# One load queue, moved warm-up matmuls and fewer weight-rest transfers in the head of a fused attention and MLP kernel

## The chip, the cores and the metric

One core of a Trainium2 chip runs one launch of the kernel. The metric is device time in microseconds (us) of that launch; lower is better. A profiled execution also has a span, from the first to the last instruction of the program; the device time of the same execution is somewhat longer than its span.

## The reference

The input x has 2048 tokens of width 448. It is layer-normalised, and the normalised xn goes two ways: through a linear attention of 16 heads (head width 28) and through a squared-ReLU MLP of width 1792. The result is x + s * silu(mlp).

```python
xn = _layernorm(x, axis=-1)
# attention
qkv = (xn @ wqkv)                      # 448 -> 3 * 448, 16 heads of 28
phi = lambda t: jnp.where(t > 0, t + 1, jnp.exp(t)) + 1e-6
pq, pk = phi(q), phi(k)
kv = jnp.einsum("bhsd,bhse->bhde", pk, v)
num = jnp.einsum("bhqd,bhde->bhqe", pq, kv)
den = jnp.einsum("bhqd,bhd->bhq", pq, z)[..., None] + 1e-6     # z: sum of pk over tokens
s = (num / den).reshape(B, S, D) @ wo
# MLP
h = xn @ w1 + b1
g = silu((relu(h) ** 2) @ w2 + b2)
return x + s * g
```

All tensors are bfloat16 in memory.

## The kernel before

The 2048 tokens are 16 tiles of 128 (names end in the tile number `si`), in four groups of four tiles (`g` = 0 to 3). The width 448 is cut into three chunks of 128 and a rest of 64; the rest chunk of a weight is kept in both partition halves (`HALF[0]`, `HALF[1]`), so that two matmuls of 64 rows can run side by side in the two halves of the array.

The code is a recorder with a planner. `add` records an operation with its reads, its writes and an estimated duration; `place` (the planner) puts the operations of ScalarE, VectorE and GpSimd in an order by its own estimate of time and picks one of eight PSUM banks for each buffer; `emit` writes the instructions with semaphore waits. TensorE (PE) and SyncE (SP) are FIXED: they run in the order of the program text. So the text order of loads is the order on SP's queue, and the order on VectorE (DVE) and ScalarE (ACT) follows from the planner's estimates, in which `prio`, `lead`, `after` and the `rate` of a load are inputs. Once emitted, every engine's order is fixed: an instruction that waits holds everything behind it on its engine.

The stage that the change touches is the first 23 us:

- **Loads.** `load_x(lo, hi)` loads token tiles into `x_tok`; `load_rows` loads 128 rows of the first 768 columns of w1 (part "w1a", chunk c); `load_rest` loads the 64 rest rows of some columns into one half; `load_main` loads the three full chunks of a column range. Parts "w1b" and "w1c" are columns 768 to 1280 and 1280 to 1792 of w1; "wk" and "wq" are the key and query columns of wqkv. The ACT queue carries b1 and the w1a rows of chunk 0, SP all the rest.
- **Norms.** For each of tiles 0 to 3: `ln_stats` (bn_stats L420 and bn_aggr L423 on DVE), `ln_rstd` (two activations on ACT, L428 and L432), `ln_norm` (DVE L438). The planner puts statistics of tile 1 ahead of the norm of tile 0 on DVE.
- **Head of the MLP.** `warm(8)` and two more `warm` calls (L990) are matmuls of ones whose result nobody reads. `tile_transpose(si)` transposes xn by PE (L482), with copies to `xT` on DVE or ACT (L490). `h_part(si, c)` (L1008) adds chunk c of tile si to six PSUM buffers, `heads[0..5]`, which hold the first six blocks of h for 512 tokens. `h_rests` (L1023) adds the rest rows, and `h_out` evacuates each head by a ReLU (ACT L606 or DVE L603).
- **Bursts.** `fours("H6 H7|H8 H9", 0)` and the like (L624 for H units, L564 for K, L588 for Q) run four units in two pairs, each pair in two PSUM banks: first four steps of the first pair, then four of the second, then three of each. H8 is block 8 of h, K0 the keys of tile 0, Q0 block 0 of the queries; a stroke, as in H3', means the next group of tokens. So H7 and H9 begin 8 matmuls after H6 and H8, and need two banks that earlier units have left.
- **Group 1.** `ln_group(1)` norms tiles 4 to 7 in two pairs, each pair followed by one DMA transpose (SP, L467) to `xT`. Its first reader on PE is H3' in `fours("Q0 Q1|Q2 H3'", 0)`, which needs all four tiles. `hold` makes statistics wait: tiles 4 and 5 for the last PE copy of tile 3, tiles 6 and 7 for the ReLU of head 2 (`relus[0, 2]`).

Of the kernel before, what the change touches and what calls it, by code (L numbers as in the profile page):

```python
# [9 lines left out]
P = 128  # L10
S, D, F = 2048, 448, 1792
# [231 lines left out]
def bass_recurrent_scan__linear_attn_block__dense_activation_squared_relu__prompt_kernel(  # L243
    nc, A_x, A_wqkv, A_wo, B_x, B_w1, B_b1, B_w2, B_b2, out
):
    with ExitStack() as es:
        sb = lambda name, shape, dtype: es.enter_context(nc.sbuf_tensor(name, shape, dtype))
        bf, f32 = dt.bfloat16, dt.float32
        pr = Program()
# [10 lines left out]
        xT = sb("xT", [P, NT, 4, P], bf)  # L260
        w_qkv = sb("w_qkv", [P, 4, 3 * D + 16], bf)
        w_1 = sb("w_1", [P, 4, F], bf)
# [6 lines left out]
        mv = sb("mv", [P, NT, 2], f32)  # L269
        rstd = sb("rstd", [P, NT], f32)  # L270
# [19 lines left out]
        FULL, HALF = slice(0, 128), (slice(0, 64), slice(64, 128))  # L290
# [51 lines left out]
        def dma(eng, dst, src, writes, nbytes, reads=(), after=(), prio=None, rate=None):  # L342
            return add(
                eng, lambda e, _: e.dma_start(dst, src), reads, writes, 0.45 if eng == "sp" else 0.5, nbytes=nbytes,
                after=after, prio=prio, mode=rate or 270e3,
            )

        def load_x(lo, hi, rate=None):
            dma(
                "sp", x_tok[:, lo:hi, :], x_r[:, lo:hi, :], [("x", i) for i in range(lo, hi)], (hi - lo) * P * D * 2,  # L350
                rate=rate,
            )

        def load_main(w, src, name, lo, hi):
            dma(
                "sp", w[:, 0:3, lo:hi], src[0:384, lo:hi].rearrange("(c p) j -> p c j", p=P), [(name, "m")],
                768 * (hi - lo),
            )

        def load_rest(eng, w, src, name, half, lo, hi, prio=None):  # L360
            dma(eng, w[HALF[half], 3, lo:hi], src[384:448, lo:hi], [(name, half)], 128 * (hi - lo), prio=prio)

        add("act", lambda e, _: e.preload_act_table_set("natural_log_exp_and_others"), [], ["actw"], 0.05, prio=-9)
        def load_rows(eng, c, prio=None, rate=None):
            dma(
                eng, w_1[:, c, 0:768], B_w1[c * P : (c + 1) * P, 0:768], [("w1a", "m", c)], 768 * 256, prio=prio,
                rate=rate,
            )

        dma("act", b1r[:, :], B_b1.rearrange("(f p) -> f p", p=P), ["b1r"], F * 2, prio=-8.5)  # L370
        load_x(0, 1)
        load_rows("act", 0, -8, rate=170e3)
        load_x(1, 2, rate=160e3)
        load_rows("sp", 1, rate=560e3)
        load_x(2, 3, rate=280e3)
        load_x(3, 4, rate=280e3)
        load_rows("sp", 2)
        load_rest("sp", w_1, B_w1, "w1a", 0, 0, 384)
        load_rest("sp", w_1, B_w1, "w1a", 1, 384, 768)
        for name, lo in (("w1b", 768), ("w1c", 1280)):  # L380
            load_main(w_1, B_w1, name, lo, lo + 512)
            load_rest("sp", w_1, B_w1, name, 0, lo, lo + 256)
            load_rest("sp", w_1, B_w1, name, 1, lo + 256, lo + 512)
            if name == "w1b":
                load_x(4, 8)
        load_main(w_qkv, A_wqkv, "wk", D, 2 * D)
        load_rest("sp", w_qkv, A_wqkv, "wk", 0, D, 2 * D)
        load_rest("sp", w_qkv, A_wqkv, "wk", 1, D, 2 * D)
        load_main(w_qkv, A_wqkv, "wq", 0, D)
        load_rest("sp", w_qkv, A_wqkv, "wq", 0, 0, D)  # L390
        load_rest("sp", w_qkv, A_wqkv, "wq", 1, 0, D)

        def load_b2():
            src = bass.AP(tensor=B_b2.tensor, offset=B_b2.offset, ap=[[0, P], [1, D]])
# [17 lines left out]
            load_rest("sp", w_qkv, A_wqkv, "wv", 1, 2 * D, 3 * D)  # L412

        masks()
        W = lambda name: [(name, k) for k in ("m", 0, 1)]


        def ln_stats(si, prio=None, after=()):
            add(
                "dve", lambda e, _: e.bn_stats(st6[:, si, :], x_tok[:, si, :]), [("x", si)], [("st", si)], 0.53 if prio is None else 0.63,  # L420
                prio=prio, after=after,
            )
            add("dve", lambda e, _: e.bn_aggr(mv[:, si, :], st6[:, si, :]), [("st", si)], [("mv", si)], 0.07, prio=prio and (0.0, 0.3, 0.3, -0.5, 2.7)[prio])  # L423
# [30 lines left out]
        def ln_group(g, lead=(1.8, 0.0), between=None):  # L454
            for a in (4 * g, 4 * g + 2):
                if a % 4 and between:
                    between()
                hold = [relus[0, 2] if a == 6 else pr.writer[("xT", 3, 1)]]
                ln_stats(a, after=hold)
                ln_stats(a + 1, after=hold)  # L460
                ln_rstd(a, a + 2)
                ln_norm(a)
                ln_norm(a + 1)
                ln_twin(a, a + 2)
                add(
                    "sp",
                    lambda e, _, a=a: e.dma_start_transpose(  # L467
                        xT[:, a : a + 2, :, :].rearrange("p s c t -> p (s c) t"),
                        xn[:, a : a + 2, :].rearrange("p s d -> p (s d)"),
                    ),  # L470
                    [(n, i) for n in ("xn", "xd") for i in (a, a + 1)], [("xT", a), ("xT", a + 1)], 1.25,
                    nbytes=2 * P * 1024, mode=180e3, lead=lead[a % 4 // 2],
                )
# [21 lines left out]
        def tile_transpose(si):  # L495
            pe_transpose([(si, 0)], [("xn", si)], xT[:, si, 0:1, :], ("xT", si, 0), ("dve", "act"), 0)
            pe_transpose([(si, 1), (si, 2)], [("xn", si)], xT[:, si, 1:3, :], ("xT", si, 1), ("act", "dve"), 0.2)
# [36 lines left out]
        def xt_names(lo, n):  # L534
            out = []
            for i in range(lo, lo + n):
                out += [("xT", i, 0), ("xT", i, 1), "xT3"] if i < 4 else [("xT", i)]
            return out
# [21 lines left out]
        def kk(si):  # L560
# [20 lines left out]

            return Unit(b, xt_names(si, 1) + W("wk"), mm, done)

        def qq(g, m):
# [8 lines left out]
            done = lambda: phi(b, pqT[:, m, g * 512 : (g + 1) * 512], ("pq", g, m), 512)  # L593
            return Unit(b, xt_names(4 * g, 4) + W("wq"), mm, done)

        relus = {}
# [20 lines left out]
        HLO, HHI = (0, 1, 2, 6, 7, 10, 11), (3, 4, 5, 8, 9, 12, 13)  # L617

        def hh(g, fi):
            b = Buf("H")  # L620
            ts = slice(4 * g, 4 * g + 4)

            def mm(e, rows, c, start, stop):
                return e.matmul(  # L624
                    ps(b)[:, 0:512].rearrange("p (s t) -> p s t", t=P), w_1[rows, c, fi * P : (fi + 1) * P],
                    xT[rows, ts, c, :], start=start, stop=stop,
                )

            part = "w1a" if fi < 6 else "w1b" if fi < 10 else "w1c"
            reads = xt_names(ts.start, ts.stop - ts.start) + [(part, 0 if fi in HLO else 1)]  # L630
            reads += [("w1a", "m", c) for c in range(3)] if fi < 6 else [(part, "m")]
            return Unit(b, reads, mm, lambda: h_out(b, g, fi))

# [351 lines left out]
        def warm(n, after=(), cols=512):  # L985
            b = Buf("W")

            def f(e, _):
                for _i in range(n):
                    last = e.matmul(ps(b)[:, 0:cols], one[:, 0:P], one[:, 0:cols], start=True, stop=True)  # L990
                return last

            add("pe", f, list(after), [b], n * cols / 1280, mode="128")
# [9 lines left out]
        def h_part(si, *chunks):  # L1003
            for c in chunks:

                def f(e, _, c=c):
                    for fi, b in enumerate(heads):
                        last = e.matmul(  # L1008
                            ps(b)[:, si * P : (si + 1) * P], w_1[:, c, fi * P : (fi + 1) * P], xT[:, si, c, :],
                            start=(si == 0 and c == 0), stop=False, skip_group_check=True,  # L1010
                        )
                    return last

                reads = [("xT", si, min(c, 1)), ("w1a", "m", c)] + (heads if si or c else [])
                add("pe", f, reads, heads, 6 * 0.056, mode="128")
# [19 lines left out]
        def b1_rows():  # L1035
            b = Buf("B1")
            add(
                "pe",
                lambda e, _: e.transpose(ps(b)[:, 0 : NF // 2].bitcast(bf), b1r[:, :], ident[0:NF, 0:NF]),
                ["b1r", "ident"], [b], 0.06, mode="128",  # L1040
            )
            add(
                "act",
                lambda e, _: e.activation(out=b1f[:, :], in_=ps(b)[:, 0 : NF // 2].bitcast(bf), func=AF.Copy), [b],
                ["b1f"], 0.15, prio=0.1,
            )

        warm(8)
        b1_rows()
        warm(4, [("mv", 0)], P)  # L1050
        warm(3, [("rstd", 0)], P)
        tile_transpose(0)
        h_part(0, 0)
        tile_transpose(1)
        h_part(0, 1)
# [8 lines left out]
        h_part(3, 0, 1, 2)  # L1064
        h_rests()
        load_w2(0, 5, [pr.writer["xT3"]])
        ln_group(1, (4.0, 4.0))
        load_w2(5, 14)
        load_b2()
        load_x(8, 12)  # L1070
# [79 lines left out]
```

## Time and profile before

| | us |
|---|---|
| median of three runs | 145.04 |
| the three runs | 144.49, 145.04, 145.11 |
| the profiled execution, device time | 144.88 |
| its span | 143.2 |
| PE busy in the span | 139.3 |
| DVE busy | 91.8 |
| ACT busy | 77.4 |
| GpSimd (POOL) busy | 27.0 |

The profile has a page and several views of one trace. In the chain of waits each line has a start, a duration, and what the end of the kernel depended on in that stretch. In the timeline each line is a run of instructions: start, duration, engine, line of the code, what is written and read, a count, and in brackets how long the engine was idle before it and what ended that. SPq and ACTq rows are issues of DMAs; PEld is the load of a matmul's stationary operand, which runs beside PE. The list of DMA issues gives size and time from issue to landing. The table by windows gives busy time and instruction count of an engine in a stretch, then the granted clock of TensorE, the busy share of the DMA engines and GB/s.

### The profile page before, as it was taken

How to read it: one execution, taken by the hardware profiler on the slowest of the kernel's cores; microseconds unless marked ns; L12 is line 12 of the kernel's file. 1: busy time of each engine (PE TensorE's matmuls, PEld its weight loads, DVE VectorE, ACT ScalarE, POOL GpSimd, SP SyncE). 2: the span in 40 equal slices, each digit the busy share in tenths (PEclk: the TensorE clock that was granted, in tenths of full speed). 3: DMA queues.
4: the chain of work that ended last, by engine and by line, in shares of the span. 5: the costliest groups of instructions: out<-in, count | busy, mean ns of one | idle time of the engine just before them, and what ended most of it. 6: DMA issues, size and time to landing. Idle time of an engine off the chain costs nothing.

```text
span 143.2 us, 3283 instructions
## 1 busy us (share of the span) xinstructions
PE 139.3 (97%) x1343; PEld 71.8 (50%) x1343; DVE 91.8 (64%) x224; ACT 77.4 (54%) x151; POOL 27.0 (19%) x46
## 2 busy tenths in 40 slices
PE   7999999999999999999999999999999999999992
PEld 2597444444554445445446444445544555554561
DVE  1757999989994655365264779700248929367963
ACT  3244999997715286527417999475179430303020
POOL 7200003514000504103200651000000005041520
PEclk9999999999999999999999999999999999999999
DMA  3889799990436000000000000013992001203242
GB/s 100 252 259 299 205 166 281 287 342 19 78 73 146 0 5 0 0 5 0 0 0 5 0 2 5 0 36 96 190 187 46 7 0 32 96 5 128 64 135 58
DMA packets 18322, 12.90 MB, mean 90 GB/s; under 512 B 7572, under 2 KB 17924, under 8 KB 18308
## 3 DMA queue, kind: packets, MB, share of 16 engines
q1 hardware_dynamic: 17060, 11.56, 29.9%
q10 hardware_dynamic: 1248, 1.15, 4.0%
q8 instruction: 10, 0.16, 0.5%
q14 instruction: 4, 0.03, 0.1%
HBM read 9.16 MB, written 1.97 MB: 78 GB/s over the span
## 4 chain that ended last, share of the span: by engine, by line
PE 94%; DMA 2%; DVE 1%; SPq 0%; issue 0%; ACT 0%
PE pb L624 27%; PE pb L877 26%; PE pb L564 7%; PE pb L686 6%; PE pb L588 6%; PE pb L947 6%; PE pb L1008 4%; PE pb L900 4%; DMA x_tok<-in_A_x_dram 2%; PE pb L974 1%; PE pb L660 1%; PE pb L691 1%; PE pb L482 1%; PE pb L817 1%; PE pb L737 1%; PE pb L842 1%
## 5 line engine op out<-in xcount | busy, mean ns | idle before, releaser
L606 ACT ACTIVATE r<-pb,b1f 128x512 bf16<-128x512 f32 x54 | 35.2, 691 | 21.0 <-PE pb L624 19.9
L624 PE MATMUL pb<-xT,w 64*128 64x512 bf16 x350 | 46.2, 376 | 0.0
L877 PE MATMUL pb<-w,r 64*128 64x448 bf16 x392 | 38.9, 349 | 0.0
L612 DVE TENSOR_TENSOR r<-r 128x512 bf16<-128x512 bf16 x40 | 17.9, 471 | 19.0 <-ACT r L606 19.0
L624 PEld LDWEIGHTS pb<-xT,w 64*128 64x128 bf16 x350 | 18.7, 94 | 19.5 <-DVE pqT L552 0.3
L877 PEld LDWEIGHTS pb<-w,r 64*128 64x128 bf16 x392 | 19.0, 94 | 18.4 <-PE pb L842 0.4
L576 POOL TENSOR_TENSOR zacc<-zacc,pk 128x448 f32<-128x448 f32 x13 | 13.7, 1050 | 47.5 <-DVE pk L552 47.0
L864 ACT ACTIVATE gbuf<-gbuf 128x448 bf16<-128x448 bf16 x15 | 8.1, 579 | 22.0 <-DVE gbuf L858 20.2
L936 POOL TENSOR_TENSOR gbuf<-gbuf,x_tok 128x448 bf16<-128x448 bf16 x7 | 7.2, 1032 | 44.1 <-DVE gbuf L932 44.0
L932 DVE TENSOR_TENSOR gbuf<-pb,gbuf 128x448 bf16<-128x448 f32 (+2 forms) x17 | 9.2, 591 | 9.0 <-PE pb L947 7.5
L564 PE MATMUL pb<-w_qkv,xT 64*128 64x448 bf16 x112 | 14.5, 349 | 0.0
L588 PE MATMUL pb<-xT,w_qkv 64*128 64x512 bf16 x84 | 14.2, 376 | 0.0
L420 DVE BATCH_NORM_STATS2 st<-x_tok 128x6 f32<-128x448 bf16 x16 | 9.5, 613 | 4.9 <-DMA x_tok<-in_A_x_dram 4.9
L613 ACT ACTIVATE r<-r 128x512 bf16<-128x512 bf16 x16 | 9.8, 633 | 0.3
L552 DVE SCALAR_TENSOR_TENSOR pk<-pb,pk 128x448 bf16<-128x448 f32 x16 | 9.4, 616 | 0.1
L686 PE MATMUL pb<-pk,xn 128*128 128x448 bf16 x48 | 9.4, 353 | 0.0
L858 DVE TENSOR_TENSOR gbuf<-pb,b2b 128x448 bf16<-128x448 f32 x15 | 8.7, 614 | 1.0 <-PE pb L877 0.6
L564 PEld LDWEIGHTS pb<-w_qkv,xT 64*128 64x128 bf16 x112 | 6.1, 94 | 5.6
L552 DVE SCALAR_TENSOR_TENSOR pqT<-pb,pqT 128x512 bf16<-128x512 f32 x12 | 8.2, 689 | 0.3
L947 PE MATMUL pb<-msb,pqT 64*128 64x448 bf16 x72 | 8.3, 349 | 0.0
L542 ACT ACTIVATE pk<-pb 128x448 bf16<-128x448 f32 x16 | 7.9, 546 | 0.5 <-PE pb L624 0.5
L588 PEld LDWEIGHTS pb<-xT,w_qkv 64*128 64x128 bf16 x84 | 5.3, 94 | 5.0 <-DVE pqT L552 0.4
(81 smaller groups left out, 123.8 us busy)
## 6 DMA issues: line engine op xcount, KB each, us to landing
out_dram<-gbuf SPq DMA_DIRECT2D x15, 112.0 KB, 1.8
x_tok<-in_A_x_dram SPq DMA_DIRECT2D x3, 448.0 KB, 8.1
w_qkv<-in_A_wqkv_dram SPq DMA_DIRECT2D x3, 336.0 KB, 7.6
w<-in_B_w_dram SPq DMA_DIRECT2D x1, 1008.0 KB, 6.1
w<-in_B_w_dram SPq DMA_DIRECT2D x2, 384.0 KB, 5.4
w_o<-in_A_wo_dram SPq DMA_DIRECT2D x1, 672.0 KB, 10.2
r<-rden_scratch SPq DMA_DIRECT2D x6, 112.0 KB
w<-in_B_w_dram SPq DMA_DIRECT2D x1, 560.0 KB, 7.5
```

The lines of the kernel that those rows point to most:

```text
L420: "dve", lambda e, _: e.bn_stats(st6[:, si, :], x_tok[:, si, :]), [("x", si)], [("st", si)], 0.53 if prio is None else 0.63,
L552: lambda e, _: e.scalar_tensor_tensor(out=slot, in0=ps(buf)[:, 0:n], scalar=1.0 + 1e-6, in1=slot, op0=ALU.add, op1=ALU.max),
L564: return e.matmul(ps(b)[:, 0:D], xT[rows, si, c, :], w_qkv[rows, c, D : 2 * D], start=start, stop=stop)
L576: return e.tensor_tensor(out=o[:, dst : dst + n], in0=first[:, src : src + n], in1=pk[:, si, src : src + n], op=ALU.add)
L588: return e.matmul(ps(b)[:, 0:512].rearrange("p (s t) -> p s t", s=4), w_qkv[rows, c, m * P : (m + 1) * P], xT[rows, 4 * g : 4 * g + 4, c, ...
L606: return e.activation(out=slot, in_=ps(b)[:, 0:512], func=AF.Relu, bias=b1f[:, fi : fi + 1])
L612: return e.tensor_tensor(out=slot, in0=slot, in1=slot, op=ALU.mult)
L613: return e.activation(out=slot, in_=slot, func=AF.Square)
L624: return e.matmul(ps(b)[:, 0:512].rearrange("p (s t) -> p s t", t=P), w_1[rows, c, fi * P : (fi + 1) * P], xT[rows, ts, c, :], start=start ...
L686: last = e.matmul(ps(b)[:, 0:D], xn[:, si, c * P : (c + 1) * P], pk[:, si, :], start=(si == 0), stop=(si == NT - 1),)
L877: last = e.matmul(ps(b)[:, 0:D], r2[si // 4][HALF[h], fi, t], w_2[HALF[h], fi, :], start=(part == 0 and fi == 0), stop=(part == 1 and fi = ...
L947: return e.matmul(ps(b)[:, 0:D], ap[c][rows, :], msb[rows, c, :], start=start, stop=stop)
```

## The change

```diff
         load_x(0, 1)
-        load_rows("act", 0, -8, rate=170e3)
-        load_x(1, 2, rate=160e3)
-        load_rows("sp", 1, rate=560e3)
+        load_x(1, 2, rate=250e3)
+        load_rows("sp", 0, rate=250e3)
+        load_rows("sp", 1, rate=330e3)
         load_x(2, 3, rate=280e3)
         load_x(3, 4, rate=280e3)
         load_rows("sp", 2)
         load_rest("sp", w_1, B_w1, "w1a", 0, 0, 384)
         load_rest("sp", w_1, B_w1, "w1a", 1, 384, 768)
-        for name, lo in (("w1b", 768), ("w1c", 1280)):
-            load_main(w_1, B_w1, name, lo, lo + 512)
-            load_rest("sp", w_1, B_w1, name, 0, lo, lo + 256)
-            load_rest("sp", w_1, B_w1, name, 1, lo + 256, lo + 512)
-            if name == "w1b":
-                load_x(4, 8)
+        load_main(w_1, B_w1, "w1b", 768, 1280)
+        for h in (0, 1):
+            src = B_w1[384:448, 768:1792].rearrange("p (b j) -> p b j", j=256)[:, h::2, :]
+            dst = w_1[HALF[h], 3, 768:1792].rearrange("p (b j) -> p b j", j=256)[:, h::2, :]
+            dma("sp", dst, src, [("w1r", h)], 128 * 512)
+        load_x(4, 8)
+        load_main(w_1, B_w1, "w1c", 1280, 1792)
         load_main(w_qkv, A_wqkv, "wk", D, 2 * D)
-        load_rest("sp", w_qkv, A_wqkv, "wk", 0, D, 2 * D)
-        load_rest("sp", w_qkv, A_wqkv, "wk", 1, D, 2 * D)
+        load_rest("sp", w_qkv, A_wqkv, "wqk", 0, 0, 2 * D)
+        load_rest("sp", w_qkv, A_wqkv, "wqk", 1, 0, 2 * D)
         load_main(w_qkv, A_wqkv, "wq", 0, D)
-        load_rest("sp", w_qkv, A_wqkv, "wq", 0, 0, D)
-        load_rest("sp", w_qkv, A_wqkv, "wq", 1, 0, D)
...
-                hold = [relus[0, 2] if a == 6 else pr.writer[("xT", 3, 1)]]
-                ln_stats(a, after=hold)
-                ln_stats(a + 1, after=hold)
+                ln_stats(a, after=[relus[0, 2] if a == 6 else pr.writer[("xT", 3, 1)]])
+                ln_stats(a + 1, after=[relus[0, 2]])
...
         warm(8)
+        warm(3, [("mv", 0)], P)
         b1_rows()
-        warm(4, [("mv", 0)], P)
-        warm(3, [("rstd", 0)], P)
+        warm(2, [("rstd", 0)], P)
         tile_transpose(0)
+        warm(3, cols=P)
         h_part(0, 0)
...
-        ln_group(1, (4.0, 4.0))
+        ln_group(1, (7.0, 5.0))
```

The names that the readers wait for follow: an H unit of w1b or w1c now waits for ("w1r", half), K and Q units wait for ("wqk", half). The w1a rows of chunk 0 move from ACT's queue to SP's, third in line. SP issues 17 loads up to and with wq instead of 19, ahead of the first part of w2. The w1 rests of both parts stand ahead of tiles 4 to 7 in the queue, and the query rests ahead of the query main part.

In the emitted order of the changed kernel, DVE runs for group 1: statistics and aggregate of tile 4, the ReLUs of heads 3 and 1, statistics and aggregate of tile 5, statistics of tiles 6 and 7, norms of tiles 4 and 5 and their copy, aggregates of 6 and 7, three squares, norms of 6 and 7 and their copy. Before, it was: statistics of 4 and 5, a ReLU, two aggregates, a ReLU, statistics of 6 and 7, two aggregates, norms of 4 and 5 and their copy, one square, norms of 6 and 7 and their copy. On ACT the second activation of tile 0's rstd now stands ahead of the copy of b1, and ACT runs four ReLUs ahead of the rstd of tiles 4 and 5 and three more ahead of that of tiles 6 and 7 (before, three, with one between the two activations, and one). The PE order differs in the warm-up matmuls alone: 3, 2 and 3 of 128 columns in place of 4 and 3. H6 and H8 now take banks 5 and 6, H7 and H9 banks 2 and 7; bank 2 held head 3, whose ReLU is the first of the two on DVE. From the first gates on, the order of all engines is nearly that of before.

More of the change, by code (lines that the diff above doesn't have):

```diff
@@ L414, in bass_recurrent_scan__linear_attn_block__dense_activation_squared_relu__prompt_kernel @@
         masks()
-        W = lambda name: [(name, k) for k in ("m", 0, 1)]
+        W = lambda name: [(name, "m")] + [("wv" if name == "wv" else "wqk", h) for h in (0, 1)]
         def ln_stats(si, prio=None, after=()):
@@ L629, in hh @@
             part = "w1a" if fi < 6 else "w1b" if fi < 10 else "w1c"
-            reads = xt_names(ts.start, ts.stop - ts.start) + [(part, 0 if fi in HLO else 1)]
+            reads = xt_names(ts.start, ts.stop - ts.start) + [(part if fi < 6 else "w1r", 0 if fi in HLO else 1)]
             reads += [("w1a", "m", c) for c in range(3)] if fi < 6 else [(part, "m")]
```

## The prediction

> **What bounds the kernel now.** The page gives the bound of the whole:
>
> ```profile
> span 143.2 us, 3283 instructions
> ...
> PE 94%; DMA 2%; DVE 1%; SPq 0%; issue 0%; ACT 0%
> ```
>
> PE carries 94% of the chain of waits, and no PE instruction behind the head goes away. So the change can only move the point from which PE runs without a break, and any later wait of PE caps that. The chain in order of time shows its start:
>
> ```profile
> 1.26 3.12 DMA x_tok<-in_A_x_dram
> ...
> 4.41 0.64 DVE st L420
> ...
> 6.20 0.82 PE pb L1008 x6
> ```
>
> Tile 1 lands at 4.38, 3.12 us after its issue; its statistics stand ahead of tile 0's norm on DVE, and from them norm, transpose and copy lead to the first h matmul at 6.20. The windows then show the clock:
>
> ```profile
> 6.20:10.03 3.83, 3.83 (x37) 1.00 0.78 223
> 10.03:12.90 2.87, 2.87 (x51) 1.00 0.90 293
> ```
>
> 37 matmuls of 128 columns take 3.83 us (104 ns each), the next 51 take 2.87 (56 ns). The granted clock says 1.00 in both, but PE runs at half rate until 10.03. The timeline shows the next place where PE could stop:
>
> ```profile
> 12.54 1.15 DVE L420 BATCH_NORM_STATS2 st<-x_tok 128x6 f32<-128x448 bf16 x2 [0.83 <-DMA x_tok<-in_A_x_dram]
> ...
> 13.61 0.73 DVE L603 TENSOR_SCALAR r<-pb,b1f 128x512 bf16<-128x512 f32 x1
> 14.26 0.24 DVE L423 BATCH_NORM_AGGREGATE mv<-st 128x2 f32<-128x6 f32 x2
> 14.40 2.72 PEld L624 LDWEIGHTS pb<-xT,w 64*128 64x128 bf16 x28 [0.30 <-DVE r L603]
> ```
>
> DVE idles until tiles 4 to 7 land (12.52), runs two statistics, then the ReLU that frees a bank for H7; that weight load goes at 14.40 and PE's 14.43 matmul follows its predecessor without a gap. **The bank arrives at the moment PE wants it.** So PE may come earlier as it likes: without an earlier landing of tiles 4 to 7, or less DVE work ahead of the ReLU, H7 stays where it is. The DMA issues have the last place, one line per transfer:
>
> ```profile
> x_tok<-in_A_x_dram SPq DMA_DIRECT2D x1, 448.0 KB, 5.9
> ...
> xT<-xn SPq DMA_TRANSPOSE x1, 3.8
> ...
> xT<-xn SPq DMA_TRANSPOSE x1, 3.3
> ```
>
> The transposes of tiles 4 to 7 are issued at 17.25 and 18.65 and land at 21.04 and 21.93; their reader H3' starts at 23.12, so 1.2 us are spare.
>
> **The change, part by part.** All against the profiled execution: 144.88 us device time, 143.2 span, so 1.7 lie outside; it stands 0.16 below the median of 145.04.
>
> *Chunk 0 of w1a behind tile 1 on SP.* Today ACT issues it at 1.51 beside tile 1 (1.26). In the landing counts of the trace, 15 of tile 1's 16 shares are in by 3.49 and one at 4.38: that one shared its DMA engine with packets of the ACT queue that took 0.63 to 0.75 us. On one queue these packets come behind it. Bounds for tile 1: 3.4 (SP's issue step of 0.46 behind tile 0's landing at 2.98) to 4.38; I take 3.5, by the 15 shares. DVE is busy with tile 0 until 3.84, so statistics of tile 1 start at 3.86 in place of 4.41: 0.55 earlier, and by the same steps (1.79 us from there) the first h matmul is ready at 5.65. Chunk 0 itself, issued at 1.73 for 1.51, lands after 3.4 us as now, 5.1 at the latest: 0.5 spare. Tiles 2 and 3, chunks 1 and 2 and the w1a rests are each issued 0.46 later; the tightest, chunk 2 (6.60, read at 8.5 now), keeps over 0.9 us.
>
> The Trainium skill, page "DMA: Bandwidth & Descriptors", section "Issuing engines are not separate DMA queues", speaks against this part: transfers from different issuers run on the same DMA engines, so that choosing the issuer saves only issue time. By it tile 1 would stay at 4.38 and the 0.55 would be 0; by the row above the late share is the shared engine's, and I keep 0.55. The sum by it is 144.9.
>
> *Warm-up matmuls.* Eight of 128 columns for seven: one more of 107 ns (the half-rate spacing, 0.93 us for 7 with starts 107 apart). The three behind tile 0's transposes run while PE would wait for the copy (0.29 us, 5.91 to 6.20 now): at half rate 3 x 0.107 = 0.32, so 0.03 longer than the cover, at full rate hidden. The one wait that moves is b1's transpose, 0.32 us later behind the three: b1 is first read at 13.34. In return ACT runs tile 0's second rstd step at 4.19 for 4.65; it is hidden, as tile 0's norm waits for tile 1's statistics.
>
> What they do to the clock this trace can't show; it shows full rate 3.83 us after the last PE gap. With gaps filled, bounds: full rate from 0.84 + 3.83 = 4.7 (gaps no longer count) to 10.03 (no effect). I take 3.83 after the last gap of the new order (at 5.04, before tile 0's transposes): 8.9. The work from 6.20 to 14.42 is 3.83 at half rate, 2.0 at full, and 4.39 at full: 6.4 us. From 5.68, with 3.2 at half rate (worth 1.67) and 4.7 left, PE would reach H7 at 13.6; bounds 12.1 (all at full rate) and 14.15 (10.03 again), against 14.42.
>
> The skill, "TensorE: Matmul & The Clock Gate", section "The HAM clock gate", has a free-running activity window of 3.4 us and warns against fitting to a cold count, since the switch moves from run to run; the 10.03 agrees with such a window. By that page my estimate is a switch anywhere from about 4.3 to 7.7 with PE full from 0.84, and PE at H7 still earlier; the bank decides all the same.
>
> *Rests in fewer transfers.* SP saves two issues (w1 rests, 0.5 to 0.6 each) behind tiles 4 to 7 and two (wqkv rests) behind "wk". But tiles 4 to 7 themselves are issued one step later (0.46, chunk 0's), behind 64 KB more of rests. Price of those 64 KB: the same amount took 0.38 today (w1b landed at 9.05, its two rests by 9.43). Most shares of tiles 4 to 7 land by 11.2, the last two at 12.48 and 12.52, one behind a single packet of 1.14 us. Landing of tiles 4 to 7: at worst 12.52 + 0.46 + 0.38 = 13.4, at best without that late packet 11.5. **I take 12.77**: the two delays overlap on the late DMA engines, which are not waiting for issues there, and part of the bad luck will not recur. Key rests: wqkv rests bring 112 KB more ahead of K0, w1 rests 64 less, so 48 KB net (0.16 at some 300 GB/s) on 16.0 plus 0.25: 16.4, needed at 17.45. Query columns land at 18.3 now, needed 22.25: hidden. The first part of w2 (20.1, read at 31.3) as well.
>
> *Statistics of one tile ahead of the ReLUs.* From the landing L: 0.02 to start, 0.66 to the aggregate, 0.10 to the ReLU's start, 0.73 for it, 0.06 to the weight load: **L + 1.57**, now L + 1.88. With 12.77 that is 14.34 against 14.40: 0.06 to 0.08 gained. This ReLU now also waits for an aggregate that waits for its statistics; behind it stand the second ReLU (its bank is read 2.2 us later) and the rest of the group's norms.
>
> *Norms of tiles 4 to 7.* By the same spacings (statistics 0.53, ReLU 0.65, aggregate 0.10, norm 0.28 and 0.39, copy 0.2, square 0.335): first transpose issued at L + 4.83 (now L + 4.74), second at L + 6.84 (now 6.13), as three squares and, on ACT, three ReLUs stand ahead. It lands 3.3 later at L + 10.1; H3' wants it at L + 1.57 + 8.70 = L + 10.3. The 1.2 us spare shrink to 0.1 or 0.2: hidden, barely. SP is held by that transpose up to about 20.9 in place of 19.95, and with it w2's second part (landed 26.1, read near 34), b2, tiles 8 to 15 (29.4 and 30.6, read at 51 and later): all spare.
>
> **Sum.** PE is at H7 by 13.6, the bank comes at 14.34 to 14.40, later waits add nothing: 0.08 gained of 144.88, so **144.8 us**, no change beyond 0.5% (0.72 us), which is about what a measurement of this kernel can tell, as its three runs lie 0.62 apart.
>
> **Rivals.**
>
> 1. *Tiles 4 to 7 land early and the clock is early.* For: only a few of 16 shares were late, one by one packet. Against: the late ones stayed late in all following loads. Landing at 11.7 puts the bank at 13.3; PE must be there by then, so full rate before about 8.3. The cap is K0 at 16.4: 1.05 of 17.45. Time 144.88 - 1.05 = 143.8. Chance 0.24.
> 2. *H3' takes the wait over, slower.* Place: the second transpose of group 1, PE at Q0. For: its slack falls from 1.2 to under 0.2, and it stands behind a ReLU on ACT that needs H7's end. Against: each step was hidden so far. It decides from an issue later than L + 7.0. If it is issued 0.5 later, lands after 3.8 as the first does now, and tiles 4 to 7 come at 13.1: 13.1 + 7.34 + 3.8 = 24.24 against 23.12, so 1.1 slower: 146.0. Chance 0.21.
> 3. *Tile 1 does not land earlier and the warm-up does nothing.* For: no row shows the late share gone, nor a switch at another time. Against: the late share waited behind packets that now come after it. PE then reaches H7 at 14.45 and the result is 144.9, inside the forecast's class. Chance 0.07; the forecast itself has 0.48.
>
> **How the numbers follow.** Within 0.5% are forecast and third rival: 0.55; faster 0.24, slower 0.21. The forecast's own range, by L from 12.4 to 13.4, is 144.4 to 145.4. The range to hold 8 in 10 reaches into both other cases, to 144.0 and 145.8.
>
> **What would show it.** Statistics of tile 1 start near 3.9 and the first h matmul near 5.7; the 56 ns spacing begins before 10; PE has a gap before H7 that ends with the DVE ReLU, 1.57 us after tiles 4 to 7 land. H3' starts within 0.3 us of the second transpose's landing. The prediction is wrong if tiles 4 to 7 land before 12.1 or after 13.5, if PE waits at K0 or H3', or if PE's idle stretch before H7 (up to 2 us) sets the clock back to half rate.

## The result and the profile after

| | before | after |
|---|---|---|
| median of 20 runs each, us | 144.92 | 146.06 |
| range, us | 143.78 to 145.62 | 144.86 to 149.48 |
| ratio, 95% interval | | 1.0059, 1.0032 to 1.0086 |
| the profiled execution, device time | 144.88 | 147.64 |
| its span | 143.15 | 145.69 |

The change makes the kernel slower: by 0.8% of the median, and by 0.6% (0.3 to 0.9) in the ratio of the table. The ratio leaves out the runs that lie apart from the others, here six runs of the changed kernel with a mean granted clock of 0.977 to 0.988 (147.17 to 149.48); the other 14, at 0.998 or more, lie from 144.86 to 146.68 with the middle at 145.75. The fall of the clock in those six runs is part of the change's price, as the windows below show; the kernel before had such a clock in 5 of the 124 runs of it beside the experiments.

The page of the changed kernel, its span and the shares of the chain of waits:

```profile
span 145.7 us, 3281 instructions
...
PE 88%; DMA 4%; SPq 4%; DVE 1%; issue 1%; ACT 0%
```

PE carries 88% of the chain in place of 94%; SP's issues and one transfer have most of the rest. In order of time (start, duration, what):

```profile
7.29 6.48 DMA x_tok<-in_A_x_dram
...
13.80 0.64 DVE st L419
...
14.46 0.18 DVE mv L422
14.64 0.65 DVE r L601
...
15.33 4.88 PE pb L622 x28
20.22 0.76 PE pb L562 x8
```

Tiles 4 to 7 are issued at 7.29 (6.66 before) and land at 13.77 (12.52). One statistics, one aggregate, one ReLU, and H7 starts at 15.33 (14.43). The 28 matmuls from H7 to K0 take 4.88 us, where 3.2 are enough at full clock (profiles below). The timeline shows what PE did until then:

```profile
5.61 0.51 PE L1006 MATMUL pb<-xT,w 128*128 128x128 bf16 x6
...
11.78 1.03 PE L622 MATMUL pb<-xT,w 64*128 64x512 bf16 x8
...
15.33 1.11 PE L622 MATMUL pb<-xT,w 64*128 64x512 bf16 x6 [2.53 <-DVE r L601]
```

The head is early, as wanted: the first h matmul at 5.61 for 6.20, the first steps of H6 and H8 done by 12.8. Then PE waits 2.53 us for the bank that the ReLU frees. The trace also has a record of the clock, whose first entry of full rate begins at 5.49. The windows of TensorE are cut every 3.413 us from there (length, busy time of PE and matmuls, granted clock, DMA share, GB/s):

```profile
2.08:5.49 3.41, 3.41 (x17) 1.00 0.86 234
5.49:8.91 3.42, 3.30 (x53) 1.00 0.76 229
8.91:12.32 3.41, 3.41 (x52) 1.00 0.89 265
12.32:15.73 3.41, 0.88 (x10) 1.00 1.05 310
15.73:19.15 3.42, 3.42 (x18) 0.50 0.45 137
19.15:22.56 3.41, 3.41 (x36) 1.00 0.34 77
```

After a stretch in which PE was busy for 0.88 of 3.41 us, the clock is at half rate for exactly one such stretch. Its 18 matmuls at half rate would have taken half as long: 1.7 us.

So the 2.84 us between this execution (147.64) and the forecast (144.8) split into three parts: H7 0.99 later than forecast (15.33 for 14.34), 1.64 more between H7 and the end of the span (130.36 for 128.72 before), and 0.22 more outside the span (1.95 for 1.73), together 2.85.

### The profile page after: what moved, and what is told of

Same layout as the page of the kernel before. It is cut to its first block, busy times and chain, and to the rows that moved or that the text cites. A ratio compares the mean times of both kernels' runs of the same rounds, so it can differ in the third digit from the quotient of the medians.

```text
span 145.7 us, 3281 instructions
## 1 busy us (share of the span) xinstructions
PE 139.5 (96%) x1344; PEld 71.2 (49%) x1344; DVE 91.7 (63%) x223; ACT 78.0 (54%) x152; POOL 27.0 (19%) x46
## 4 chain that ended last, share of the span: by engine, by line
PE 88%; DMA 4%; SPq 4%; DVE 1%; issue 1%; ACT 0%
PE pb L622 27%; PE pb L875 26%; PE pb L562 7%; PE pb L684 6%; PE pb L586 6%; PE pb L945 5%; DMA x_tok<-in_A_x_dram 4%; SPq L344 4%; PE pb L898 4%; PE pb L972 1%; PE pb L658 1%; PE pb L689 1%; PE pb L815 1%; PE pb L735 1%; PE pb L840 1%
## 5 line engine op out<-in xcount | busy, mean ns | idle before, releaser
L622 PE MATMUL pb<-xT,w 64*128 64x512 bf16 x350 | 48.1, 388 | 2.5 <-DVE r L601 2.5
L622 PEld LDWEIGHTS pb<-xT,w 64*128 64x128 bf16 x350 | 19.4, 96 | 23.2 <-DVE r L601 3.0
L574 POOL TENSOR_TENSOR zacc<-zacc,pk 128x448 f32<-128x448 f32 x13 | 13.6, 1048 | 47.9 <-DVE pk L550 47.4
L611 ACT ACTIVATE r<-r 128x512 bf16<-128x512 bf16 x17 | 10.3, 639 | 0.2
L427 ACT ACTIVATE rstd<-mv,eps 128x2 f32<-128x2 f32 (+1 forms) x10 | 3.0, 299 | 9.0 <-DVE mv L422 7.3
```

The source lines that it names most:

```text
L574: return e.tensor_tensor(out=o[:, dst : dst + n], in0=first[:, src : src + n], in1=pk[:, si, src : src + n], op=ALU.add)
L611: return e.activation(out=slot, in_=slot, func=AF.Square)
L622: return e.matmul(ps(b)[:, 0:512].rearrange("p (s t) -> p s t", t=P), w_1[rows, c, fi * P : (fi + 1) * P], xT[rows, ts, c, :], start=start ...
```

## The experiments

Three theories went in. **A**: the landing of tiles 4 to 7 (L) sets H7 through the DVE chain, L plus 1.57 in the changed order and L plus 1.88 in the old one; L is late since these tiles are issued later and behind 64 KB more of rests, and a long idle stretch costs the clock. **B**: the cap is behind, the second transpose of group 1 and H3', so that the ordering of norms and squares is what costs. **C**: all of the loss is the clock that falls back.

**Taking the wait away in four ways.** Each edits the changed kernel:

```diff
relufirst: statistics of tile 4 wait for the ReLUs of heads 1 and 3
-  after=[relus[0, 2] if a == 6 else pr.writer[("xT", 3, 1)]]
+  after=[relus[0, 2] if a == 6 else pr.writer[("xT", 3, 1)]] + [relus[0, i] for i in (1, 3) if a == 4]
xfirst: tiles 4 to 7 ahead of the two merged w1 rests
   load_main(w_1, B_w1, "w1b", 768, 1280)
+  load_x(4, 8)
...
-  load_x(4, 8)
both: relufirst and xfirst together
warmgap: six matmuls of 512 columns, read by nobody, ahead of H6
+  warm(6)
   fours("H6 H7|H8 H9", 0)
```

> The changed kernel, with the statistics of tile 4 held until the ReLUs of heads 1 and 3. Theory A (H7's bank is freed by a DVE ReLU that stands behind the statistics of tile 4, so behind the landing of tiles 4 to 7): PE runs from H6 into H7 without a gap, next stops at K0 for the key rests (16.6 to 16.8 in the trace of the changed kernel, where K0 started at 20.2), and never falls back to half rate; 144.5 to 145.2 us. Theory B (the second transpose of group 1 is the cap): PE stops at H3' until that transpose lands near 23.5 to 24, as it does not depend on the ReLUs; 145.4 to 146.0 us. Theory C (all of the loss is the clock that falls back): as A, at most 144.5 us.

> The changed kernel, with tiles 4 to 7 ahead of the two w1 rests in the queue. Theory A: tiles 4 to 7 land about 0.4 us earlier than in the changed kernel (64 KB and the two issues, 13.0 to 13.4 for 13.8 in its trace), and H7 follows by 1.57 us; 145.0 to 145.6 us. Theory B: H7 moves, the end does not, as the transposes cap it: 145.6 to 146.0. Rival to both: the landing is set by late DMA engines, whatever stands ahead: about 13.8 again and 146 us.

> The changed kernel with both edits: statistics of tile 4 behind the ReLUs, tiles 4 to 7 ahead of the w1 rests. Theory A: no stop at H7, a stop at K0 for the key rests of up to 1 us, the second transpose 0.4 us earlier than with the first edit alone: 144.2 to 144.9 us. Theory B: 145 us or more, with the stop at H3'.

> The changed kernel, with six more warm-up matmuls of 512 columns (1.3 us at full rate) between the head's rests and H6. Theory A: H7 still starts 1.57 us after tiles 4 to 7 land, but PE's idle time before it shrinks from 2.7 to 1.4 us, so that the clock stays at full rate: no run above 146.5, median 145.2 to 145.6 us. Theory C (clock alone): 144.5 us or less. If the idle time does not set the clock back: the same spread as the changed kernel, 144.9 to 149.5.

| | median, us | range | ratio to before, 95% interval |
|---|---|---|---|
| relufirst | 146.08 | 145.06 to 146.77 | 1.0089, 1.0056 to 1.0122 |
| xfirst | 143.79 | 143.19 to 145.13 | 0.9930, 0.9898 to 0.9961 |
| both | 144.55 | 144.12 to 146.12 | 1.0001, 0.9971 to 1.0031 |
| warmgap | 147.13 | 146.13 to 148.32 | 1.0150, 1.0119 to 1.0181 |

xfirst, one line moved, turns the loss into a gain, a larger one than theory A gave it (145.0 to 145.6, with a landing at 13.0 to 13.4). Its chain of waits:

```profile
5.97 5.72 DMA x_tok<-in_A_x_dram
...
12.63 0.65 DVE r L601
...
13.33 3.19 PE pb L622 x28
```

Issued at 5.97 (7.29 in the changed kernel), landed at 11.69, H7 at 13.33, and 28 matmuls at full rate. That is the mechanism of theory A; its size was missed, since A counted 64 KB and two issues as 0.4 us, and the issue alone came 1.32 earlier. The next bound shows in the same trace, at H6:

```profile
12.20 2.16 PE L622 MATMUL pb<-xT,w 64*128 64x512 bf16 x16 [0.39 <-DMA w<-in_B_w_dram]
```

PE now waits there for the merged rests of w1, which stand behind tiles 4 to 7 (the second landed at 12.16). The kernel both has the same wait (0.89 us), and one of 0.98 for the key rests at K0; its 144.55 is what A gave it (144.2 to 144.9).

relufirst took H7's dependence on L away and earned nothing (146.08 for A's 144.5 to 145.2), which A had not priced; its timeline has two other waits:

```profile
15.42 1.04 PE L622 MATMUL pb<-xT,w 64*128 64x512 bf16 x8 [0.80 <-DMA w<-in_B_w_dram]
...
17.38 0.93 PE L562 MATMUL pb<-w_qkv,xT 64*128 64x448 bf16 x8 [0.91 <-DMA w_qkv<-in_A_wqkv_dram]
```

PE reaches H10 and waits for w1c (landed 15.29), then K0 and waits for the key rests (17.29): the loads behind tiles 4 to 7 are late with them. A third wait, 0.47 us for a bank, stands at Q (29.62). The three make 2.2 us, and none is at H3', where theory B put it. warmgap missed outright. It had no gap at H7 and no half rate in any run, and was slower still; its fastest run was profiled, and its chain ends with

```profile
29.17 0.70 DVE pqT L550
...
29.91 1.04 PE pb L586 x8
```

The planner, which counts the extra matmuls, had put ACT and DVE into another order, and Q there waits for a bank 17.49 us after L (12.42). In c_after below, whose plan has no filler, the same unit starts 16.50 after L. So a filler on PE doesn't isolate the idling: it moves the plan too. Theory C falls by the runs that the clock left alone: 14 of the changed kernel with their middle at 145.75, 0.8 above before, and all six of relufirst.

**Part by part.** The next kernels replace the six transposes by DMA with plain copies of the same 256 KB, so that the tiles behind them arrive untransposed (c_before, c_after); on c_before stand the one-queue part alone (c_queue), the merged rests alone (c_rests), the warm-up matmuls alone (c_warm) and the order of statistics alone (c_norms).

```diff
c_before, c_after
-  e.dma_start_transpose(xT[:, a : a + 2, :, :].rearrange("p s c t -> p (s c) t"), ...
+  e.dma_start(xT[:, a : a + 2, :, :].rearrange("p s c t -> p (s c t)"), ...
```

> The kernel before, with each of its six DMA transposes replaced by a plain copy of the same 256 KB to the same place, so that the group's tiles arrive untransposed; all orders stay. It is the base for the single parts that follow. The copies land sooner than the transposes' 3.3 to 3.8 us. Theory A (the wait at H7 for the landing of tiles 4 to 7): nothing before H3' changes, 144.5 to 145.0 us.

> The changed kernel with the same copies in place of transposes. Theory A: the loss against c_before stays, 0.6 to 1.4 us, as it arises at H7. Theory B (the transposes of group 1 are the cap): the loss goes, within 0.4 us of c_before.

> The kernel before with copies for transposes and the one-queue part alone. Theory A: tile 1 lands near 3.5, the first h matmul starts near 5.7, but tiles 4 to 7 are issued 0.46 us later and H7 waits for them: 0 to 0.6 us slower than c_before. If the issue step costs nothing: 0.2 to 0.4 us faster.

> The kernel before with copies for transposes and the merged rests alone (64 KB more ahead of tiles 4 to 7, 112 KB of query rests ahead of K0). Theory A: tiles 4 to 7 land later and H7 with them: 0.3 to 0.9 us slower than c_before. If fewer issues pay instead: not slower than c_before.

> The kernel before with the plain copies of c_before, and of the change only the warm-up matmuls. Theory A: H7 waits for the bank, 1.88 us after tiles 4 to 7 land, and these matmuls move no load: within 0.3 us of c_before, 144.3 to 144.9. Rival 1, PE's head or the switch of its clock is the bound: 144.0 or less. Rival 2, the warm-up matmuls delay tile 0's copy and with it the first h matmul: 145.0 or more.

> The kernel before with the plain copies of c_before, and of the change only the order of the statistics (one tile instead of two ahead of the ReLU). Theory A: H7 starts 1.57 us after tiles 4 to 7 land in place of 1.88, and PE waited 1.0 us for it in c_before's profile, so 0.2 to 0.3 faster than c_before: 144.2 to 144.4. Rival, the later norms of tiles 4 to 7 or another wait take it back: no faster than c_before, 144.5 to 145.5.

| | median, us | ratio, 95% interval | profiled | L | H7 | span end less H7 | outside the span, mean of runs |
|---|---|---|---|---|---|---|---|
| before | | | 144.88 | 12.52 | 14.43 | 128.7 | 1.74 |
| c_before | 144.53 | 0.9970, 0.9951 to 0.9988 | 144.50 | 12.13 | 14.02 | 128.8 | 1.74 |
| c_warm | 144.78 | 0.9990, 0.9965 to 1.0016 | 144.06 | 11.69 | 13.57 | 128.7 | 1.73 |
| c_norms | 144.96 | 0.9995, 0.9972 to 1.0019 | 145.20 | 13.00 | 14.56 | 128.9 | 1.75 |
| c_queue | 145.80 | 1.0095, 1.0058 to 1.0131 | 145.57 | 13.06 | 15.14 | 128.7 | 1.74 |
| c_rests | 145.28 | 1.0022, 1.0001 to 1.0043 | 147.97 | 13.59 | 15.47 | 130.4 | 2.04 |
| c_after | 147.29 | 1.0125, 1.0074 to 1.0175 | 145.52 | 12.86 | 14.42 | 129.0 | 2.05 |
| after | 146.06 | 1.0059, 1.0032 to 1.0086 | 147.64 | 13.77 | 15.33 | 130.4 | 1.99 |

Theory B falls, though not by the copies alone. With them the loss is not smaller: 2.8 us of median, above A's 0.6 to 1.4, as three of the six runs of c_after had the clock set back. But the two copies of group 1 took 3.0 and 2.5 us from issue to landing in c_after, the transposes 2.9 and 2.7 in the changed kernel, so that they hardly move the cap that B names. What speaks against B is that in no profile PE idles at H3'.

The table accounts for each profiled run: the device time is L, plus the DVE chain, plus 128.7 to 129.0 to the end of the span, plus 1.7 where the clock falls back, plus what lies outside the span. The 129.0 of c_after holds a wait of 0.21 us at K0 for the key rests, which landed at 17.78 there. The chain is 1.88 in the old order, 1.56 to 1.57 with one tile's statistics, and 2.08 in c_queue, where the planner put both aggregates ahead of the ReLU:

```profile
13.08 1.15 DVE L420 BATCH_NORM_STATS2 st<-x_tok 128x6 f32<-128x448 bf16 x2 [2.90 <-DMA x_tok<-in_A_x_dram]
...
14.15 0.30 DVE L423 BATCH_NORM_AGGREGATE mv<-st 128x2 f32<-128x6 f32 x2
14.37 1.38 DVE L603 TENSOR_SCALAR r<-pb,b1f 128x512 bf16<-128x512 f32 x2
...
15.14 0.61 PE L624 MATMUL pb<-xT,w 64*128 64x512 bf16 x4 [2.08 <-DVE r L603]
```

The one-queue part alone costs most (1.3 us of median, where 0 to 0.6 was expected), with two clusters: six runs from 145.32 to 145.80 at full clock and five from 147.06 to 147.55 with 0.986 to 0.988, which is 1.7 apart. The middle of the six is 145.58, so 1.05 of the 1.3 is lost at full clock; 0.2 of that is the longer chain, which the changed kernel doesn't have. The merged rests alone cost 0.75, as expected (0.3 to 0.9). They show the same fall of the clock in their profile; their windows, cut as above:

```profile
9.76:13.17 3.41, 3.30 (x44) 1.00 0.96 284
13.17:16.58 3.41, 1.11 (x12) 1.00 1.02 284
16.58:20.00 3.42, 3.42 (x20) 0.50 0.21 72
```

The warm-up matmuls are worth nothing that shows. c_norms shows its H7 at L plus 1.56, but the 0.2 to 0.3 that theory A gave it does not appear in the times: 144.96 lies in the range of the rival. L, which no part of c_norms moves, scatters from 11.69 to 13.00 in the four kernels with the old loads and may hide it; that isn't shown.

**Clock and queue order once more.** c_fill puts seven idle matmuls of 512 columns between the first steps of H6 and H8 and those of H7 in c_after; c_xfirst is the line of xfirst in c_after; c_xact gives c_xfirst the old first loads back.

```diff
c_fill: in the burst of H6 to H9, after the first four steps of H6 and H8
+  if fill and j == 1:
+      warm(fill)
c_xact: on c_xfirst
-  load_x(1, 2, rate=250e3)
-  load_rows("sp", 0, rate=250e3)
-  load_rows("sp", 1, rate=330e3)
+  load_rows("act", 0, -8, rate=170e3)
+  load_x(1, 2, rate=160e3)
+  load_rows("sp", 1, rate=560e3)
```

> The changed kernel with the six transposes by DMA replaced by plain copies of the same bytes (so the tiles behind them arrive untransposed), as in c_after, and seven filler matmuls of 512 columns (read by nobody) between the first four steps of H6 and H8 and those of H7 and H9, where PE idles 1.6 to 2.5 us in the profiles of the changed order. Theory A with the clock: idling of over about 2 us before H7 is what sets the clock back to half rate for 3.41 us and costs 1.7 us in some runs; with the filler no run loses it, so all lie at the lower cluster of c_after, 145.3 to 146.4, with one clock of at least 0.997 in all of them. Rival: the clock falls back for another reason (a later gap, the granted power): then runs 1.5 us or more apart remain, as in c_after (145.5 to 145.9 beside 147.1 to 148.1). If the filler itself is longer than the idling, H7 starts later than 1.57 us after tiles 4 to 7 land, and the excess is added.

> c_after with one edit: tiles 4 to 7 are issued ahead of the two rests of w1b and w1c, not behind them. Theory A: they land about 1 us earlier than in c_after (11.7 to 12.4), H7 starts 1.57 us later, PE idles less than 1.2 us there and the clock never falls back: 143.5 to 144.3. Rival, the last DMA engines are late whatever stands ahead of these tiles: landing 12.8 or later and a time like c_after's, 145.5 to 147.5.

> c_xfirst with one edit: the rows of chunk 0 of w1a go back to ACT's queue, ahead of tile 1, so SP issues one load less in the head. Theory A: tiles 4 to 7 land 0.4 to 0.6 earlier still (10.5), but H7's bank is no longer the bound there; tile 1 lands up to 0.6 later, PE's first h matmul starts at 5.6 to 6.2, so it is equal or up to 0.5 slower than c_xfirst: 143.7 to 144.2. Rival, the extra issue on SP still delays something that PE waits for (rests of w1, key rests): 0.3 or more faster, 143.4 or less.

c_fill ran at 147.22 (146.17 to 148.0), ratio 1.0163 (1.0119 to 1.0207): no run below a mean clock of 0.998, where c_after had three of six at 0.988. Six runs alone would be few. But of all runs with the loads of the changed kernel, 14 of 34 had the clock set back where PE idles at H7 (the changed kernel, c_after), and 0 of 18 where a filler or the order of the ReLUs shortens that idling (warmgap, c_fill, relufirst); with tiles 4 to 7 moved up it is 0 of 71. So the idling does set the clock. The range of times was missed, since Q waits for its bank 17.49 us after L again (14.12 to 31.61), as in warmgap. c_xfirst ran at 143.70, ratio 0.9928 (0.9904 to 0.9951), as expected; the chain of its PE has no break at all where H7 stands:

```profile
11.10 0.75 PE pb L1021 x6
11.86 3.96 PE pb L622 x36
15.81 0.76 PE pb L562 x8
```

c_xact is the same within the error, 143.96 and 0.9933 (0.9904 to 0.9961). Its tiles 4 to 7 land at 10.68 for 10.98, its tile 1 at 4.60 for 3.37, and its first h matmul starts at 6.35 for 5.60. The one-queue part earns nothing measurable even where it costs nothing.

**The changed kernel again.** Its first profile fell in a run with the clock set back, so it was run as it is three more times.

> The changed kernel itself, for a profile of a run in which the clock does not fall back (14 of its 20 timed runs, 144.9 to 146.7). Theory A: device time is the start of H7 plus 130.4 to 130.8, as in every other profile without the fall-back, so at 145.75, the middle of these runs, tiles 4 to 7 land at 13.4 to 13.6, H7 starts 1.57 later at 15.0 to 15.2, and PE waits nowhere else before 30 us. Rival: they land at 12.8 or so, as taken in the prediction, and 0.5 us or more is lost at another wait (K0, H3', Q). If the clock does fall back, 147 or more, it repeats the first profile.

> The changed kernel itself once more, for a profile of a run in which the clock does not fall back. The expectations of the first try stand: by theory A the device time is the start of H7 plus 130.4 to 130.8, so that at 145.0 to 146.5 H7 starts at 14.4 to 15.9, 1.57 after tiles 4 to 7 land, and PE waits nowhere else before 30 us; by the rival they land by 12.8 and another wait (K0, H3', Q) takes 0.5 us or more. If the clock falls back, 147 or more.

> As again2, the same kernel once more: a second chance of a profile at full clock.

The three profiled executions took 148.1, 147.59 (both at half rate for 3.41 us) and 145.51. The last one, at full clock, has this chain:

```profile
7.32 5.59 DMA x_tok<-in_A_x_dram
...
12.93 0.64 DVE st L419
...
14.47 3.20 PE pb L622 x28
17.66 0.76 PE pb L562 x8
```

L 12.91, H7 1.56 later, no wait at K0 or after. PE idled 1.6 us there, 2.2 to 2.9 us in the three others. The device time of 145.51 is 131.0 more than the start of H7, 0.2 above what was expected: that rest is outside the span, 2.16 us here. In the four profiles of the changed kernel L is 12.91, 13.52, 13.77 and 14.05. Four more kernels have the same loads ahead of these tiles: 12.42 (warmgap), 12.86 (c_after), 13.75 (relufirst) and 14.12 (c_fill). The mean of the eight is 13.43; that of the four kernels with the old loads is 12.34.

**What lies outside the span.** In every kernel with separate rests the device time exceeds the span by 1.67 to 1.81 us; with merged rests the mean is 1.95 to 2.07 in every kernel with six runs or more. It is no fixed step: single runs with merged rests lie from 1.68 to 2.23, and three of the five last runs of the changed kernel at 1.70 to 1.74. So two kernels take the transfers of xfirst apart again: split has the eight separate rests of before, w1merged only the four of the key and query columns.

```diff
split, on xfirst (w1merged: the last two additions alone)
-  for h in (0, 1): ... dma("sp", dst, src, [("w1r", h)], 128 * 512)
+  load_rest("sp", w_1, B_w1, name, 0, lo, lo + 256)
+  load_rest("sp", w_1, B_w1, name, 1, lo + 256, lo + 512)
...
-  load_rest("sp", w_qkv, A_wqkv, "wqk", h, 0, 2 * D)
+  load_rest("sp", w_qkv, A_wqkv, "wk", h, D, 2 * D)
+  load_rest("sp", w_qkv, A_wqkv, "wq", h, 0, D)
```

> xfirst with the 64-row rests in the eight transfers of before (four of w1, four of the key and query columns), so none merged; tiles 4 to 7 still ahead of every rest of w1b and w1c. In the runs so far the device time exceeds the span by 1.67 to 1.81 us in every kernel with separate rests and by 1.95 to 2.07 on average in every kernel with merged ones. Theory M, the merged transfers cost it: 1.73 to 1.76 outside the span here, and 0.2 to 0.3 faster than xfirst (143.79) if the span stays, 143.4 to 143.6. Rival, it comes from the other parts together: 1.95 or more outside the span, and 143.8 to 144.3.

> xfirst with only the key and query rests back in four transfers; the two merged rests of w1 (of two blocks each, a strided source of 512 bytes a row and block) stay. Theory M1, the strided w1 rests cost the 0.25 outside the span: 1.95 or more here. Theory M2, the wider wqk rests cost it: 1.73 to 1.76 here. Times 143.4 to 144.1 by either.

split: 143.28 (142.96 to 144.95), ratio 0.9916 (0.9884 to 0.9949), 1.74 outside the span in the mean. w1merged: 143.54 (143.21 to 144.35), ratio 0.9908 (0.9881 to 0.9936), 1.81 outside. xfirst has 1.95, so merging costs there 0.21 us in all, 0.14 of it by the two wide transfers of key and query rests; w1merged lies between its two theories (1.95 or more, 1.73 to 1.76). By what means isn't shown: nothing in the trace covers that time. split has the lowest median of all kernels run, and xfirst, split and w1merged beat both kernels; split's ratio and those of the other two overlap.

## Why the prediction was wrong

- **Bound and mechanism: right.** The bank of H7 comes L plus 1.57 in the forecast and 1.56 to 1.57 in all four profiles; PE waits there and at no later point up to 30 us.
- **Head of PE: the times right, the reason in part wrong.** Tile 1 landed at 3.38 to 3.77 for 3.5, the first h matmul at 5.61 for 5.65 in all four. Yet tile 1 landed at 3.34, 3.35 and 3.61 in three kernels with chunk 0 still on ACT's queue (c_norms, c_warm, c_rests), at 4.08 to 4.60 in the other three, and at 3.33 to 3.92 in the fourteen profiles with one queue: the late share that the prediction took for lasting comes and goes. That it shared an engine with ACT's long packets isn't shown either: they had ended by 3.61, and the trace doesn't name a packet's engine. And the one queue alone doesn't give 5.65. In the four kernels on c_before's base that keep the old warm-up matmuls (c_before, c_norms, c_rests, c_queue) the first h matmul is at 5.94, since ACT has tile 0's second rstd step behind the copy of b1, at 4.65, and the norm waits for it:

```profile
4.88 0.40 DVE L438 TENSOR_SCALAR xn<-x_tok,mv,rstd 128x448 bf16<-128x448 bf16 x1 [0.23 <-ACT rstd L432]
```

  That is c_queue. The prediction had called this step hidden; it is worth 0.33 us of the head as soon as tile 1 is early. In c_warm, with the moved matmuls and the old loads, the first h matmul is at 5.61.
- **First full rate: earlier than taken.** It began at 5.49 to 6.21 for 8.9 (three profiles have a record of it), which lies inside the prediction's other estimate, 4.3 to 7.7. The moved matmuls are not needed for it (5.66 in c_before without them, 6.53 in c_warm with them). PE had its first steps of H6 and H8 done by 12.8 for 13.6. Being early earned nothing: it lengthened the idling.
- **Landing of tiles 4 to 7: the step that failed.** Taken: 12.77, that is 0.25 of the 0.84 us of delay that the prediction itself had summed (0.46 and 0.38), since "the two delays overlap on the late DMA engines" and "part of the bad luck will not recur". Measured: 12.91 to 14.05, three of four above the upper bound of 13.4; with the four other kernels of the same loads seven of eight are later than 12.77. The delays add. The issue came 0.63 later, not 0.46: 0.47 for chunk 0, and 0.16 more as the two merged rests hold SP for 0.65 and 0.61 (up to the query columns and their rests SP issues 18 loads in place of 21, and the three are saved behind these tiles). With 0.38 for the 64 KB that makes 1.01, and the mean L of eight profiles is 1.09 later than that of four with the old loads.

  Of the landing counts, the eighth of 16 came at 11.12 for 10.36, and the last at 13.77 for 12.52; eleven had landed by 11.52, five came from 12.84 on. In c_fill 15 shares were in by 12.25 and the last came at 14.12.

  At full clock the forecast was missed by 0.95 us (145.75 for 144.8); as an estimate, the mean landing is 0.66 of that (13.43 for 12.77), and what lies outside the span 0.25. c_xfirst, with tiles 4 to 7 ahead of the merged rests, takes it all back.
- **The clock: named as a danger, not priced.** The forecast saw an idle stretch of "up to 2 us"; with L 0.7 to 1.3 us later than taken it was 2.2 to 2.9 in three profiles, and the clock was set back for 3.41 us, 1.7 us lost. That happened in 6 of 20 runs, and in 5 of the 8 later ones. It lifts the median of the 20 from 145.75 to 146.06.
- **Outside the span: assumed constant at 1.7.** It grew by 0.2 to 0.3 in the mean, with the merged transfers.
- **Second transpose and H3' (rival 2): the working holds, the rival doesn't.** In the profile at 145.51 the transpose is issued at L plus 6.79 (forecast 6.84), lands at L plus 9.5 (forecast 10.1, as it took 2.7 us and not 3.3), and H3' starts at L plus 10.6: 1.1 spare. Key rests landed at 16.72 there for 16.4, and PE came to K0 at 17.66. That the rival's time of 146.0 is the measured median is chance.
- **Rival 1 described xfirst, not this change**: with tiles 4 to 7 at 11.69 its forecast of 143.8 is the measured 143.79. That the two agree so closely is chance in part: the cap that the rival names, the key rests at K0, does not act there (K0 follows H7 without a wait, at 16.52).

The Trainium skill, page "DMA: Bandwidth & Descriptors", section "Issuing engines are not separate DMA queues", was weighed against the row of tile 1's late share. What I drew from the page, that tile 1 would stay at 4.38, was too narrow, and so was my reading of the row: with two queues tile 1 landed at 3.34 to 4.60, with one at 3.33 to 3.92. The page's statement that the choice of the issuer saves only issue time fits the times: here the move costs issue time on SP (0.47 us), and c_xact, which takes it back, runs at 143.96 against 143.70.

## What to carry to other kernels

When the first wait behind a head is a bank or a tile that hangs on a landing, the order on the issuing queue is the lever: here each transfer put ahead of it cost its issue and its bytes in full. Merging transfers saves issues only behind the merged ones; what stands ahead of the critical load should be the fewest bytes and the least issue time, not the fewest transfers. Because one landing scatters by over 1 us, a forecast from one trace should add the delays to the mean of several profiles, not to the one at hand. And a head made earlier without an earlier landing turns into idling, which can be dearer than the wait itself when it takes the clock down.

## What was not expected of the hardware

- **The clock is decided in fixed stretches of 3.413 us.** All full-rate records from the first switch on are whole multiples of it (10.24 is three). A stretch with 0.84, 0.88, 1.11 or 1.23 us of PE work is followed by half rate (four profiles), one with 1.80, 1.85, 2.09 or 2.43 isn't (c_after, relufirst, c_norms, c_before). The stretch of c_after:

```profile
11.30:14.71 3.41, 1.80 (x18) 1.00 1.04 301
```

  So whether an idling of 2 us or more costs 1.7 us depends on whether it falls into one stretch or across two, which changes from run to run; that fits the clusters 1.7 apart. The Trainium skill, "TensorE: Matmul & The Clock Gate", section "The HAM clock gate", has this window as free-running, and the records agree; its rule, in "HAM oscillation — how this bites in real kernels", warns of idle gaps over about 3.4 us, and here 2.2 to 2.9 were enough.
- **The first switch seems to need a nearly full stretch.** In the profile before, the stretch with the small gaps did not do, the next did:

```profile
3.20:6.62 3.42, 3.12 (x19) 1.00 0.84 256
6.62:10.03 3.41, 3.41 (x35) 1.00 0.81 238
```

  The switch came at 10.03 there, and at 4.0 to 6.5 in the twelve other profiles with a record; in xfirst a stretch with 3.16 us was enough. One profile on each side, 0.04 us apart, is thin evidence for a bound.
- **Merged transfers cost 0.2 to 0.3 us outside the span**, in most runs, where no instruction runs (1.74 against 2.04 in the mean, c_before and c_rests; 1.74 against 1.95, split and xfirst).
- **The landing of one 448 KB transfer scatters by over 1 us** with the same code, set by the last one to five of its 16 shares.
